# Attention's opening written out by hand: loads in order of need, block means spread by VectorE

## The chip, the core and the metric

The program runs on one core of a Trainium2 chip. A core has TensorE (PE: weight loads and matmuls), VectorE (DVE), ScalarE (ACT), GpSimd (POOL) and SyncE (SP), which here only issues transfers; 16 DMA engines move data between the device's memory and the on-chip buffers (SBUF; matmuls write to PSUM). The metric is the device time of one execution in microseconds (us), as a median over runs.

## The reference

Three layers in a row, in float32. The first is attention of 2 batches, 8 heads, 768 positions, 64 values per head, in which each query sees its near keys and one summary per block of 32 keys:

```
k_sum = k.reshape(B, H, nb, block, D).max(axis=3)
v_sum = v.reshape(B, H, nb, block, D).mean(axis=3)
scores_l = where(|i - j| < 16, scale * q @ k.T, -1e9)
scores_s = scale * einsum('bhsd,bhnd->bhsn', q, k_sum) + log(block)
a = softmax(concatenate([scores_l, scores_s], axis=-1))
out = a @ concatenate([v, v_sum], axis=2)
```

Its output goes through a mixture of 8 experts, of which each token takes its best (`relu(x @ w1[e]) @ w2[e]`, times a gate), and then through `(x @ w_a * (x @ w_b)) @ w_out`.

## The kernel before

Heads are taken two at a time: a **pair** p is 128 partitions of keys, and there are 8 pairs, p0 to p7 (4 for each batch). A pair's 768 queries are 12 windows of 64; four windows are a **quad**, so there are 24 quads, 0 to 23. Of the first batch, quads 0 to 2 belong to p0, 3 to 5 to p1, then p2 and p3 alternate (6, 8, 10 and 7, 9, 11); the second batch repeats this with p4 to p7 from quad 12 on.

A pair needs four loads, all issued on SP's queue: `kr` (keys, 400 KB), `qd` (queries, 384 KB), `vbt` (values laid out for block sums, 390 KB) and `vt` (values by window, 585 KB, 96 of 120 rows). They have 3, 3, 2 and 3 buffers. From `kr`, `key_blocks` takes the maxima over blocks of 32 (tile `ks`, one VectorE reduction). From `vbt`, `value_sums` makes sums in three additions on GpSimd, `value_blocks` turns them into means (one small matmul into `o`, a VectorE copy into `vs`), and `fill_v` spreads the 24 rows of `vs` over the 12 windows of `vt`, rows 96 to 119, by a DMA of 24 x 12 pieces of 520 bytes that SP issues.

A quad i then goes through: `windows` (three copies into `kt`: ScalarE from `kr`, VectorE from `kr`, VectorE or GpSimd from `ks`), `scores` (matmuls s<-kt,qd: s(i)), `largest` (four VectorE pieces, mask and maximum, in the trace the operation CUSTOM_DVE_ANT_0; the mask lies in `cs`), `exps` (ScalarE), `turn` (transposes into `pst`, ScalarE copy into `pt`), `values` (matmuls o<-vt,pt) and `norm` (three VectorE instructions, rs, rs and x). The results of `values` and of `value_blocks` share two PSUM buffers; scores have three, transposes two.

The order on each engine is the order in which the code calls these helpers (a manual schedule). `step(n)` interleaves stages of several quads: in step n, windows of quad n+3, norm of n-2, exps of n+1, scores and largest of n+2, turn of n and values of n-1; helpers of pairs and loads are called in the steps ahead of the pair's first quad. Engines and queues work their own instructions off in order, so an instruction that waits holds what stands behind it on its engine. When a group of quads is done, its rows are turned and routed (px, pl, prb), and the expert stage begins as soon as its tokens are known.

Of the kernel before, what the change touches and what calls it, by code (L numbers as in the profile page):

```python
# [10 lines left out]
F32 = mybir.dt.float32  # L11
# [7 lines left out]
ALU = mybir.AluOpType  # L19
AX = mybir.AxisListType  # L20
# [81 lines left out]
def fused_kernel(  # L102
# [276 lines left out]
    krs, qs, vbs, kss, vss, kts, vts, prs, nms, pts, os_, xt2 = ({} for _ in range(12))  # L379
    qds = [big.tile([P, QW, NWIN], F32, name=f"qd{i}") for i in range(NQD)]  # L380

    def load_k(p):
        kr = krs[p] = k_p.tile([P, S + 32], F32, name="kr")
        nc.sync.dma_start(kr, k[p])

    def load_vb(p):
        vbt = vbs[p] = v_p.tile([KW, 8, 2 * VW], F32, name="vbt", bufs=2)
        nc.sync.dma_start(vbt, vb[p])

    def load_q(p):  # L390
        qd = qs[p] = qds[len(qs) % NQD]
        nc.sync.dma_start(qd, q[p].rearrange("h d q n -> (h d) q n"))

    def load_v(p):
        vt = vts[p] = v_p.tile([KC, NWIN, 2 * VW], F32, name="vt")
        nc.sync.dma_start(vt[0:KW], v[p])

    def fill_v(p):
        nc.sync.dma_start(vts[p][KW:KC], vss[p][KW:KC].to_broadcast([NBLK, NWIN, 2 * VW]))

    n1 = CCOL["first"][1]
    nc.scalar.dma_start(cs[:, :n1], cst[:, :n1])

    zrow = big.tile([P, KD], F32, name="zrow")
    nc.gpsimd.memset(zrow, 0.0)
    nc.gpsimd.dma_start(xs[0:1, :].rearrange("a (p c) -> (a p) c", p=P), zrow)

    oh = r1.tile([P, NT, E], BF16, name="oh")
    unit = r1.tile([P, NT], F32, name="unit")
# [8 lines left out]

    def key_blocks(p):
        ks = kss[p] = s_p.tile([P, NBLK], F32, name="ks")  # L420
        nc.vector.tensor_reduce(
            out=ks, in_=krs[p][:, 16:16 + S].rearrange("p (m i) -> p m i", i=32), op=ALU.max, axis=AX.X)

    def value_sums(p):
        vbt = vbs[p]
        for r in (4, 2, 1):
            nc.gpsimd.tensor_tensor(out=vbt[:, 0:r], in0=vbt[:, 0:r], in1=vbt[:, r:2 * r], op=ALU.add)

    def value_blocks(p):
        o = ps_c.tile([P, 512], F32, name="o", tag="c")  # L430
# [42 lines left out]
    def exps(i):  # L473
        for w in range(4):
            nc.scalar.activation(prs[i][:, w, :], prs[i][:, w, :], AF.Exp, scale=-1.0, bias=nms[i][:, w:w + 1])
# [377 lines left out]
    def step(n):  # L853
        def ok(i):
            return 0 <= i < NQ

        def due(ahead):

            m = n + ahead
            return begin.get(0 if m == 1 else m) if m else None  # L860

        win = windows(n + 3) if ok(n + 3) else iter(())
        nrm = norm(n - 2) if ok(n - 2) else iter(())
        for ops in 3 * (win, nrm):
            next(ops, None)
        if ok(n + 1):
            exps(n + 1)
        if ok(n + 2):
            scores(n + 2)
            largest(n + 2)  # L870
        if n + 5 in begin:
            key_blocks(begin[n + 5])
        if due(3):
            value_sums(due(3))
        if ok(n):
            turn(n)
        if ok(n - 1):
            values(n - 1)
        if due(2):
            value_blocks(due(2))  # L880
        if due(1):
            fill_v(due(1))
        for ahead, load in ((5, load_q), (5, load_vb), (3, load_v), (7, load_k)):
            if n + ahead in begin:
                load(begin[n + ahead])
        for fn in todo.pop(n, []):
            fn()

    def wi(j):
        return lambda n: widx[:, j, n:n + 1]  # L890

    with tc.manual_schedule():
        for n in range(-7, NQ + 2):
            step(n)
            if n == 4:
                nc.scalar.dma_start(cs[:, n1:], cst[:, n1:])
                nc.scalar.dma_start(wg_sb, wg)
            if n == 8:
                nc.vector.tensor_copy(tri, cc("tri"))
# [350 lines left out]
```

## Time and profile before

| | us |
|---|---|
| median of 3 runs | 584.59 (583.51 to 589.82) |
| the profiled execution, its own time | 580.55 |
| its span in the trace | 578.8 |
| TensorE busy in the span | 542.7 (94%) |
| VectorE, ScalarE, GpSimd busy | 364.5, 245.9, 210.7 |

Attention and its routing fill about the first 100 us of the span, experts the stretch to 260 us, the last layer the rest. The trace is of the profiled execution; its own time lies 1.75 us above its span, and 4.04 us below the median of the runs.

### The profile page before, as it was taken

What the parts mean: (1) busy time and instruction counts of PE and PEld (TensorE: products, weight loads), DVE (VectorE), ACT (ScalarE), POOL (GpSimd) and SP (SyncE); (2) the same over time, 40 slices, a digit from 0 to 9 for tenths busy, and PEclk for the clock granted to TensorE, in tenths of its full rate; (3) what the DMA queues carried; (4) which work ended last, traced back from release to release, by engine and by line L of the source; (5) the groups of instructions that cost most, each with busy time, mean ns of one, the idle gap of its engine ahead of it and who ended that gap; (6) DMA issues with size and microseconds to landing.
All of it is one profiled execution on the core that took longest, in us unless ns stands there. A gap on an engine that the chain in (4) does not pass through costs nothing.

```text
span 578.8 us, 9146 instructions
## 1 busy us (share of the span) xinstructions
PE 542.7 (94%) x3358; PEld 451.7 (78%) x3358; DVE 364.5 (63%) x908; ACT 245.9 (42%) x516; POOL 210.7 (36%) x189
## 2 busy tenths in 40 slices
PE   4899976987979999999999999999999999999996
PEld 3678765967878997987778878888788888888885
DVE  3766676775767878777655766676667666342321
ACT  3667756345655655564422332233223322222321
POOL 3332337326164654740015334533453345200000
PEclk9999999999999999999999999999999999999999
DMA  8999883049684938554313231323132312020202
GB/s 255 253 218 278 219 302 148 8 176 336 247 310 172 375 131 323 207 230 166 124 37 109 74 107 39 109 74 106 40 110 72 108 39 74 1 74 0 74 0 74
DMA packets 24288, 83.88 MB, mean 145 GB/s; under 512 B 2864, under 2 KB 5424, under 8 KB 20656
## 3 DMA queue, kind: packets, MB, share of 16 engines
q1 hardware_dynamic: 13984, 38.16, 22.9%
q0 software_dynamic: 6944, 38.80, 17.6%
q10 hardware_dynamic: 3312, 6.29, 3.1%
q8 instruction: 28, 0.46, 0.3%
q14 instruction: 20, 0.16, 0.1%
HBM read 69.72 MB, written 12.32 MB: 142 GB/s over the span
## 4 chain that ended last, share of the span: by engine, by line
PE 50%; DVE 2%; DMA 1%; SPq 1%; ACT 0%; issue 0%; POOL 0%; POOLq 0%; DVEq 0%
PE pa L1124 11%; PE pa L1126 11%; PE pa L1125 11%; PE po L1156 6%; PE po L1157 6%; PE po L1155 6%; DMA yg<-ya 1%; PE px L988 1%; SPq L977 1%; DVE yg L978 0%; DVE c_top L1031 0%; DVE yw L990 0%; POOL yw L1032 0%; ACT yw L989 0%; DVE c_top L1024 0%
## 5 line engine op out<-in xcount | busy, mean ns | idle before, releaser
L1124 PE MATMUL pa<-yw,abh 128*128 128x512 f32 x288 | 113.7, 395 | 0.3 <-DVE yw L990 0.3
L1126 PE MATMUL pa<-yw,abl 128*128 128x512 f32 x288 | 112.6, 391 | 0.0
L1125 PE MATMUL pa<-yw,abh 128*128 128x512 f32 x288 | 112.2, 390 | 0.0
L1029 POOL TENSOR_TENSOR c_rest<-c_rest,c_ex 128x512 f32<-128x512 f32 x36 | 51.7, 1448 | 127.1 <-DVE c_ex L1028 126.4
L205 DVE TENSOR_TENSOR w<-w,w 128x512 fp32r<-128x512 f32 x100 | 69.1, 735 | 5.2 <-ACT w L204 3.5
L1126 PEld LDWEIGHTS pa<-yw,abl 128*128 128x128 f32 x288 | 54.0, 188 | 12.1
L1124 PEld LDWEIGHTS pa<-yw,abh 128*128 128x128 f32 x288 | 54.2, 188 | 11.5 <-DVE yw L990 0.5
L1125 PEld LDWEIGHTS pa<-yw,abh 128*128 128x128 f32 x288 | 54.1, 188 | 11.4
L277 PE MATMUL ph<-xh,w 128*128 128x256 f32 x192 | 55.0, 286 | 6.9 <-DVE hl L281 4.4
L204 ACT CAST w<-w 128x512 fp32r<-128x512 f32 x100 | 56.4, 619 | 3.9 <-DVE w L205 3.9
L1156 PE MATMUL po<-yw,gh 128*128 128x512 f32 x144 | 56.9, 395 | 0.2
L1155 PE MATMUL po<-yw,gh 128*128 128x512 f32 x144 | 56.2, 390 | 0.0
L1157 PE MATMUL po<-yw,gl 128*128 128x512 f32 x144 | 56.1, 390 | 0.0
L278 PE MATMUL ph<-xl,w 128*128 128x256 f32 x192 | 54.0, 281 | 0.0
L279 PE MATMUL ph<-xh,w 128*128 128x256 f32 x192 | 53.8, 280 | 0.0
L455 PE MATMUL s<-kt,qd 64*64 64x120 f32 x384 | 34.6, 324 | 9.5 <-DMA qd<-in_q 7.7
L277 PEld LDWEIGHTS ph<-xh,w 128*128 128x128 f32 x192 | 36.2, 189 | 9.1 <-DVE hl L281 5.4
L253 PE MATMUL py<-w,hh 128*128 128x512 f32 x104 | 41.0, 395 | 1.1 <-DVE w L205 1.1
L252 PE MATMUL py<-w,hh 128*128 128x512 f32 x104 | 41.8, 402 | 0.0
L1110 DVE TENSOR_TENSOR gl<-gt,gh 128x512 fp32r<-128x512 f32 x24 | 16.5, 691 | 40.0 <-ACT gh L1109 38.0
L1014 ACT ACTIVATE c_rest<-raw 128x512 f32<-128x512 uint32 x36 | 23.1, 670 | 42.8 <-POOL abl L1032 42.8
L254 PE MATMUL py<-w,hl 128*128 128x512 f32 x104 | 40.9, 393 | 0.0
(200 smaller groups left out, 1034.4 us busy)
## 6 DMA issues: line engine op xcount, KB each, us to landing
raw<-in_wab SPq DMA_DIRECT2D x22, 512.0 KB, 3.6
raw<-in_wc SPq DMA_DIRECT2D x12, 512.0 KB, 3.5
vt<-in_v SPq DMA_DIRECT2D x8, 585.0 KB, 8.7
kr<-in_k SPq DMA_DIRECT2D x8, 400.0 KB, 7.4
vbt<-in_vb SPq DMA_DIRECT2D x8, 390.0 KB, 9.7
qd<-in_q SPq DMA_DIRECT2D x8, 384.0 KB, 8.1
xs<-x ACTq DMA_DIRECT2D x12, 256.0 KB, 3.4
yg<-ya SPq DMA_DIRECT2D x8, 256.0 KB, 2.6
```

The source lines that it names most:

```text
L204: nc.scalar.copy(a[:, c], r[:, c])
L205: nc.vector.tensor_tensor(out=l[:, c], in0=r[:, c], in1=f(a[:, c]), op=ALU.subtract)
L277: nc.tensor.matmul(ph, a, xh[:, c, :], start=(c == 0), stop=False)
L278: nc.tensor.matmul(ph, a, xl[:, c, :], start=False, stop=False)
L279: nc.tensor.matmul(ph, l, xh[:, c, :], start=False, stop=(c == KD - 1))
L1029: nc.gpsimd.tensor_tensor(out=rest, in0=rest, in1=ex.bitcast(F32), op=ALU.mult)
L1124: nc.tensor.matmul(pa, a, yh[:, c, :], start=(c == 0), stop=False)
L1125: nc.tensor.matmul(pa, a, yl[:, c, :], start=False, stop=False)
L1126: nc.tensor.matmul(pa, l, yh[:, c, :], start=False, stop=(c == KD - 1))
L1155: nc.tensor.matmul(po[g][i], a, bh, start=(fc == 0), stop=False)
L1156: nc.tensor.matmul(po[g][i], a, bl, start=False, stop=False)
L1157: nc.tensor.matmul(po[g][i], l, bh, start=False, stop=(fc == KF2 - 1))
```

## The change

The steps -7 to 2, in which the pipeline filled by itself, give way to a function `prologue` that calls the helpers one by one, and the loop begins with step 3, in which `step` leaves out the norm and values that are done by then. In it:

- the load of p0's keys is cut in two, and so is the reduction of its block maxima;
- SP issues kr, qd and the constants `cs` of p0 first (`cs` came on ScalarE's queue), then vbt and vt of p0, then p1's loads;
- quads 0, 1, 2 are scored one after the other and go through turn and values before quad 3 is scored; `value_sums` of p0 is done by VectorE;
- `fill_v` is, for all 8 pairs, a VectorE copy of 24 x 1560 elements with a repeated source;
- the row of zeros that GpSimd writes out is made on one partition (1 x 512) and no longer on 128 (128 x 4).

```diff
-    def load_k(p):
+    def load_k(p, *at):
         kr = krs[p] = k_p.tile([P, S + 32], F32, name="kr")
-        nc.sync.dma_start(kr, k[p])
+        for a, b in zip((0, *at), (*at, S + 32)):
+            nc.sync.dma_start(kr[:, a:b], k[p][:, a:b])
...
     def fill_v(p):
-        nc.sync.dma_start(vts[p][KW:KC], vss[p][KW:KC].to_broadcast([NBLK, NWIN, 2 * VW]))
+        nc.vector.tensor_copy(vts[p][KW:KC], vss[p][KW:KC].to_broadcast([NBLK, NWIN, 2 * VW]))
...
-    nc.scalar.dma_start(cs[:, :n1], cst[:, :n1])
-
-    zrow = big.tile([P, KD], F32, name="zrow")
+    zrow = big.tile([1, DM], F32, name="zrow")
     nc.gpsimd.memset(zrow, 0.0)
-    nc.gpsimd.dma_start(xs[0:1, :].rearrange("a (p c) -> (a p) c", p=P), zrow)
+    nc.gpsimd.dma_start(xs[0:1, :], zrow)
...
     def key_blocks(p):
         ks = kss[p] = s_p.tile([P, NBLK], F32, name="ks")
-        nc.vector.tensor_reduce(
-            out=ks, in_=krs[p][:, 16:16 + S].rearrange("p (m i) -> p m i", i=32), op=ALU.max, axis=AX.X)
+        n = 1 if start[p] else 2
+        for i in range(n):
+            a, b = S // n * i, S // n * (i + 1)
+            nc.vector.tensor_reduce(
+                out=ks[:, a // 32:b // 32], in_=krs[p][:, 16 + a:16 + b].rearrange("p (m i) -> p m i", i=32),
+                op=ALU.max, axis=AX.X)
...
-            nc.gpsimd.tensor_tensor(out=vbt[:, 0:r], in0=vbt[:, 0:r], in1=vbt[:, r:2 * r], op=ALU.add)
+            (nc.gpsimd if start[p] else nc.vector).tensor_tensor(out=vbt[:, 0:r], in0=vbt[:, 0:r], in1=vbt[:, r:2 * r], op=ALU.add)
...
+    def prologue():
+
+        p0, p1, p2, p3 = list(start)[:4]
+        load_k(p0, 16 + S // 2)
+        load_q(p0)
+        nc.sync.dma_start(cs[:, :n1], cst[:, :n1])
+        load_vb(p0)
+        load_v(p0)
+        load_k(p1)
+        load_q(p1)
+        load_vb(p1)
+        load_k(p2)
+        load_v(p1)
+        key_blocks(p0)
+        for i in range(3):
+            list(windows(i))
+        for i in range(2):
+            scores(i)
+            largest(i)
+            exps(i)
+        value_sums(p0)
+        scores(2)
+        largest(2)
+        turn(0)
+        value_blocks(p0)
+        fill_v(p0)
+        turn(1)
+        exps(2)
+        values(0)
+        turn(2)
+        list(norm(0))
+        values(1)
+        key_blocks(p1)
+        list(windows(3))
+        values(2)
+        list(norm(1))
+        scores(3)
+        largest(3)
+        list(windows(4))
+        exps(3)
+        value_sums(p1)
+        scores(4)
+        largest(4)
+        value_blocks(p1)
+        key_blocks(p2)
+        list(windows(5))
+        fill_v(p1)
+        load_k(p3)
+        for p in (p2, p3):
+            load_q(p)
+            load_vb(p)
+
     with tc.manual_schedule():
-        for n in range(-7, NQ + 2):
+        prologue()
+        for n in range(3, NQ + 2):
+            if n == 4:
+                key_blocks(list(start)[3])
             step(n)
```

SP's queue, its first transfers, before (the number behind a tile's name is that of the tile made; kr_148, qd0, vbt_153 and vt_161 are p0's; vt_161<-vs_215 is the spreading of p0's means):

```order
L384 DMA kr_148<-in_k 128x800
L392 DMA qd0_131<-in_q 128x768
L388 DMA vbt_153<-in_vb 96x1040
L384 DMA kr_155<-in_k 128x800
L396 DMA vt_161<-in_v 96x1560
L392 DMA qd1_132<-in_q 128x768
L388 DMA vbt_188<-in_vb 96x1040
L384 DMA kr_217<-in_k 128x800
L399 DMA vt_161<-vs_215 24x12x130
L396 DMA vt_253<-in_v 96x1560
L384 DMA kr_255<-in_k 128x800
```

The same queue now (kr_147, qd0, vbt_152 and vt_154 are p0's; L900 is the load of the constants):

```order
L385 DMA kr_147<-in_k 128x400 x2
L393 DMA qd0_131<-in_q 128x768
L900 DMA cs_60<-in_cst 128x512
L389 DMA vbt_152<-in_vb 96x1040
L397 DMA vt_154<-in_v 96x1560
L385 DMA kr_156<-in_k 128x800
L393 DMA qd1_132<-in_q 128x768
L389 DMA vbt_159<-in_vb 96x1040
L385 DMA kr_161<-in_k 128x800
L397 DMA vt_163<-in_v 96x1560
```

The spreading of p0's means no longer stands ahead of p1's vt, the constants stand third, and p0's vt ahead of p1's keys.

TensorE's first matmuls before (s_167, s_198, s_227 are quads 0 to 2, s_265 and s_318 are 3 and 4; o<-vbt is a pair's block means, o<-vt,pt are a quad's values):

```order
L455 MATMUL s_167<-kt_157,qd0_131 64x120 x8
L455 MATMUL s_198<-kt_163,qd0_131 64x120 x8
L431 MATMUL o_213<-vbt_153,cs_60 24x130
L455 MATMUL s_227<-kt_190,qd0_131 64x120 x8
L480 MATMUL pst_245<-cs_60,pr_176 120x128 x4
L455 MATMUL s_265<-kt_219,qd1_132 64x120 x8
L480 MATMUL pst_282<-cs_60,pr_207 120x128 x4
L491 MATMUL o_289<-vt_161,pt_250 64x65 x8
L431 MATMUL o_298<-vbt_188,cs_60 24x130
L455 MATMUL s_318<-kt_257,qd1_132 64x120 x8
```

And now (s_180, s_199, s_221 are quads 0 to 2, s_309 and s_335 are 3 and 4):

```order
L458 MATMUL s_180<-kt_168,qd0_131 64x120 x8
L458 MATMUL s_199<-kt_172,qd0_131 64x120 x8
L458 MATMUL s_221<-kt_176,qd0_131 64x120 x8
L483 MATMUL pst_236<-cs_60,pr_189 120x128 x4
L434 MATMUL o_243<-vbt_152,cs_60 24x130
L483 MATMUL pst_248<-cs_60,pr_208 120x128 x4
L494 MATMUL o_259<-vt_154,pt_241 64x65 x8
L483 MATMUL pst_268<-cs_60,pr_230 120x128 x4
L494 MATMUL o_280<-vt_154,pt_253 64x65 x8
L494 MATMUL o_295<-vt_154,pt_273 64x65 x8
L458 MATMUL s_309<-kt_291,qd1_132 64x120 x8
L458 MATMUL s_335<-kt_324,qd1_132 64x120 x8
```

All of p0's transposes and values stand ahead of quad 3's scores now; from quad 6 on the row is the one of before.

VectorE where p3's means are copied out, between the maxima of quad 7 and of quad 8, before:

```order
L433 COPY vs<-o 24x130
L500 TENSOR_SCALAR rs<-o 128x4
L443 COPY kt<-kr 128x4x32
L502 RECIPROCAL rs<-rs 128x4
L504 TENSOR_TENSOR x<-o,rs 128x2x128
L462 ISA pr,nm<-s,cs 128x120
```

And now:

```order
L436 COPY vs<-o 24x130
L400 COPY vt<-vs 24x1560
L503 TENSOR_SCALAR rs<-o 128x4
L446 COPY kt<-kr 128x4x32
L505 RECIPROCAL rs<-rs 128x4
L507 TENSOR_TENSOR x<-o,rs 128x2x128
```

The copy that spreads a pair's means (here p2's) stands ahead of a quad's norm, whose last instruction frees the PSUM buffer that the next values write to.

## Rows read from the trace of the kernel before

**Rows 1.** The span in stretches: busy time of each engine, clock, DMA.

```profile
core 0: us, PE busy (x) PEld busy (x) DVE busy (x) ACT busy (x) POOL busy (x), PEclk, DMA share, GB/s
0.00:7.70 7.70, 0.00 (x0) 0.02 (x1) 1.58 (x6) 2.30 (x4) 1.36 (x7) 1.00 0.76 242
...
14.10:24.40 10.30, 9.83 (x131) 8.17 (x130) 8.99 (x51) 8.05 (x24) 3.12 (x6) 1.00 1.01 246
24.40:32.20 7.80, 5.18 (x56) 3.71 (x56) 2.44 (x19) 3.79 (x11) 5.43 (x10) 0.78 1.03 250
32.20:67.30 35.10, 35.10 (x471) 28.99 (x470) 25.33 (x155) 25.95 (x75) 7.92 (x12) 1.00 1.01 254
67.30:84.00 16.70, 12.28 (x164) 10.50 (x162) 10.99 (x75) 8.72 (x25) 6.30 (x7) 1.00 0.70 232
```

**Rows 2.** TensorE in order of time, 7 to 38 us: start, duration, [idle before <-releaser].

```profile
7.71 3.50 PE L455 MATMUL s<-kt,qd 64*64 64x120 f32 x32 [7.71 <-DMA qd<-in_q]
...
14.10 1.33 PE L455 MATMUL s<-kt,qd 64*64 64x120 f32 x16
15.36 0.65 PE L480 MATMUL pst<-cs,pr 128*120 128x128 f32 x4
...
26.16 0.71 PE L491 MATMUL o<-vt,pt 120*64 120x65 f32 x16 [1.80 <-DMA vt<-vs]
...
27.59 1.89 PE L455 MATMUL s<-kt,qd 64*64 64x120 f32 x16
29.41 1.11 PE L480 MATMUL pst<-cs,pr 128*120 128x128 f32 x4
...
34.75 1.35 PE L455 MATMUL s<-kt,qd 64*64 64x120 f32 x16
```

**Rows 3.** All engines in order of time, 0 to 30 us.

```profile
5.26 0.95 DVE L421 TENSOR_REDUCE ks<-kr 128x24 f32<-128x768 f32 x1 [4.24 <-DMA kr<-in_k]
...
6.13 0.22 DVE L443 COPY kt<-kr 128x128 f32<-128x128 f32 x1
...
9.64 0.28 DVE L462 CUSTOM_DVE_ANT_0 pr<-s,cs 128x120 f32<-128x120 f32 x1 [2.98 <-PE s L455]
...
10.46 0.95 DVE L421 TENSOR_REDUCE ks<-kr 128x24 f32<-128x768 f32 x1
...
14.28 2.60 POOL L427 TENSOR_TENSOR vbt<-vbt 96x520 f32<-96x520 f32 x3 [2.44 <-DMA vbt<-in_vb]
...
14.45 1.21 DVE L443 COPY kt<-kr 128x128 f32<-128x128 f32 x1
```

**Rows 4.** SP's issues of transfers in order of time.

```profile
12.70 1.00 SPq L399 DMA_DIRECT2D vt<-vs  x1
...
57.29 0.83 SPq L399 DMA_DIRECT2D vt<-vs  x1
...
58.80 0.52 SPq L388 DMA_DIRECT2D vbt<-in_vb  x1
```

**Rows 5.** DMA, 14 to 16 us.

```profile
DMA packets 346, 0.34 MB, mean 168 GB/s; under 512 B 20, under 2 KB 308, under 8 KB 346
```

**Rows 6.** DMA, 9 to 13 us.

```profile
DMA packets 329, 1.09 MB, mean 273 GB/s; under 512 B 43, under 2 KB 43, under 8 KB 329
```

**Rows 7.** DMA, 0 to 6 us, in 40 slices of 0.15 us.

```profile
GB/s 0 0 0 0 0 0 0 0 0 0 0 85 85 107 128 212 274 280 167 280 280 342 385 266 414 383 463 383 405 480 349 437 413 420 382 408 388 347 326 194
```

**Rows 8.** VectorE's instructions by line and shape: busy us, mean ns.

```profile
L205 DVE TENSOR_TENSOR w<-w,w 128x512 fp32r<-128x512 f32 x100 | 69.1, 735 | 5.2 <-ACT w L204 3.5
...
L1022 DVE TENSOR_SCALAR c_ex<-raw 128x512 int32<-128x512 int32 x36 | 15.1, 420 | 0.0
...
L504 DVE TENSOR_TENSOR x<-o,rs 128x256 f32<-128x256 f32 x24 | 10.2, 424 | 0.4
...
L433 DVE COPY vs<-o 24x130 f32<-24x130 f32 x8 | 2.4, 300 | 6.9 <-PE o L431 6.8
L445 DVE COPY kt<-ks 128x96 f32<-128x96 f32 x13 | 2.3, 180 | 0.0
```

**Rows 9.** TensorE in order of time, 64 to 102 us.

```profile
71.25 0.40 PE L431 MATMUL o<-vbt,cs 96*24 96x130 f32 x2 [1.36 <-POOL vbt L427]
```

More of the change, by code (lines that the diff above doesn't have):

```diff
@@ L862, in step @@
         win = windows(n + 3) if ok(n + 3) else iter(())
-        nrm = norm(n - 2) if ok(n - 2) else iter(())
+        nrm = norm(n - 2) if n > 3 and ok(n - 2) else iter(())
         for ops in 3 * (win, nrm):
@@ L876, in step @@
             turn(n)
-        if ok(n - 1):
+        if n > 3 and ok(n - 1):
             values(n - 1)
```

## The prediction

> **What bounds the kernel now.** The table of stretches comes first [rows 1]. From 32.2 to 67.3 us TensorE is busy all 35.10 us at full clock: there attention runs at TensorE's pace, and nothing that another engine or a transfer saves counts. Before that it isn't so: nothing until 7.7 us, 9.83 of 10.30 us from 14.1, and only 5.18 of 7.80 from 24.4, at a granted clock of 0.78. After it, 12.28 of 16.70. So the change can win in the first 32 us and behind 67 us, and what it wins there moves everything behind it, since experts and last layer start from attention's rows.
>
> TensorE in order of time says what ends each pause [rows 2]. Its first matmul starts at 7.71 us, when the queries have landed. At 26.16 it has stood 1.80 us for `vt<-vs`, the DMA that spreads p1's means. Behind that pause the clock is low: s and pst of a quad take 1.89 and 1.11 us against 1.33 and 0.65 at 14.1, so 1.0 us is lost again. At 71.25 it has stood 1.36 us for the block sums of the last pair [rows 9].
>
> The DMA engines' share is 1.0 from 14 to 67 us at 246 to 254 GB/s [rows 1], against 273 GB/s from 9 to 13 us [rows 6]. Over 14 to 16 us, while p0's spreading runs in its 288 pieces of 520 bytes, 0.34 MB move at 168 GB/s [rows 5]; at 273 it would be 0.55. One spreading so costs the loads about 0.8 us; there are eight. SP waits too: its spreading goes out at 12.70, after p0's means exist, and all later loads stand behind it [rows 4].
>
> **The change part by part.**
>
> *Start.* The bytes moved by time follow from the slices [rows 7]: 0.41 MB by 3.5 us, 0.67 MB by 4.2, 0.80 MB by 4.5. Before, keys and constants (0.67 MB together) share the engines and VectorE starts on the keys at 5.26 [rows 3], some 1.0 us after their last byte. Alone on the engines, the first half of the keys (0.2 MB, 2.9 us) would be usable at 3.9, the second at 4.5, the queries at 5.5. VectorE then needs half of 0.95 us for the second half's maxima and 0.22 us each for two copies: quad 0's scores start at 5.6 us in place of 7.71, 2.1 us sooner. If the early rate is a ramp that sharing has nothing to do with, it is 7.0.
>
> *First quads.* I walk the new order with durations of rows. At the start TensorE takes 1.75 us per quad of scores (3.50 for two [rows 2], against 1.33 later): quads 0 to 2 end at 10.8. VectorE has finished quad 1's maxima at 10.0 (four pieces take 0.82 us, 9.64 to 10.46 [rows 3]). It then makes p0's block sums: 520, 260 and 130 columns of two SBUF sources, by 0.735 us for 512 [rows 8] and in proportion about 1.45 us; quad 2's maxima to 12.3; the means' copy 0.30 [rows 8]; the spreading.
>
> *The spreading's price* isn't in the trace: 1560 elements from one source. Such copies take 0.18 us for 96 elements and 0.42 for 512 [rows 8], 0.58 ns an element: 1.0 us. The block maxima take 0.95 us for 768 elements [rows 3], by which it would be 1.9. I take 1.0, since the copy is of the first kind, and keep 1.9 as the bound. On the other side DMA and SP lose eight transfers.
>
> So the spreading ends at 13.65, quad 0's values (0.71 [rows 2]) at 14.4, its norm (0.75, of which the multiplication is 0.42 [rows 8]) at 15.4, p1's maxima (0.95) at 16.3, a copy into kt: quad 3 is scored at 16.7, where before it was 14.10 [rows 2]. The code then alternates: maxima of quad 3 (0.9) and the copy for quad 4 (0.22) stand ahead of quad 4's scores (19.3); maxima of 4, a means' copy (0.30), p2's maxima (0.95) and a copy stand ahead of quad 5's (22.9). TensorE stands 4.9 us in pieces from 11 to 23 us. From quad 6 on (24.8) it is fed: 28.1 for quad 7, 30.9 for quad 8, 33.9 for quad 9 with half a microsecond for values that wait till VectorE, late from p2's spreading, has freed their PSUM buffer. Before, quad 9 is at 34.75 [rows 2], and from here on both orders are alike. The 2.1 us of the start, the 1.80 of the spreading's DMA and the 1.0 of the low clock go into the serial opening; 0.85 us are left.
>
> *Middle.* VectorE is busy 25.33 of 35.10 us [rows 1]; p2's to p6's spreadings make it 30.3, so TensorE stays the bound (at 1.9 us each 34.8, which is just full).
>
> *Last pair.* SP held the last block sums' load until 58.80, behind a spreading that went out at 57.29 [rows 4]. Without eight spreadings at 0.8 us and that hold it lands some microseconds sooner, and the 1.36 us wait [rows 9] goes. Next late is VectorE, with two spreadings more in 67 to 84 us (10.99 of 16.70 busy [rows 1]): I charge 0.4 us. For clock lost in the pauses from 11 to 23 us I charge 0.3, a third of one low stretch of 1.0; zero and two stretches are the bounds.
>
> The rest has one answer: the larger zero row and the constants' place on SP cost nothing, since the mask is first used at 9.64 [rows 3], after the constants' bytes have long moved.
>
> Sum: -0.85 - 1.36 + 0.4 + 0.3 = -1.5 us. Against the profiled execution's 580.55 that is 579.0; the runs' median lies 4.04 above it, so **583.1**.
>
> **Rivals.**
>
> *VectorE and GpSimd keep each other out: slower.* At 14.45 a VectorE copy of 128 elements takes 1.21 us beside a GpSimd addition that began at 14.28, where the same copy took 0.22 at 6.13 [rows 3]; it stays until 15.66, while the additions run. The spreadings are such copies, and the new block sums on GpSimd run in the same stretch. If those of p1, p2 and p3 each wait 1.0 us where VectorE is already the chain (22 to 34 us), the sum turns to +1.5: **586.1**. It decides once two of them coincide with an addition. For it: p2's additions and p1's spreading both become ready at about 23 us. Against: a pair's own additions are over before its spreading. The Trainium skill says of this (SBUF — State Buffer, "SBUF: two separate sides") that VectorE and GpSimd share one pair of ports under an exclusive lock, held for a whole instruction. The row at 14.45 agrees with 1.21 us against 0.22.
>
> *The copy is slow: no change.* At 1.9 us the first spreading is 0.9 later on the chain, p2's and p3's stretch TensorE's wait by another 0.8, and VectorE, full in the middle, costs some 0.3: -1.5 + 2.0 = +0.5, **585.1**. Against it stand the two copies' rows. The Trainium skill (VectorE: DVE Perf Modes, "The perf-mode tier table") gives float32 copies within SBUF two elements a cycle; by that the price would be about 0.9 us, as the rows have it.
>
> *The order of loads brings nothing: no change.* If the first bytes come no faster alone, the start gives 0.7 and not 2.1: -0.1, **584.5**. For it: only 85 to 280 GB/s move until 3 us [rows 7], though two queues have work.
>
> *Everything fits: faster.* If no low stretch comes and GpSimd's and VectorE's pieces interleave without the half microsecond, and the clock also holds in 67 to 101 us: -0.85 - 0.5 - 1.36 - 1.5 = -4.2, **580.4**; with the start's waits of 4.9 us a third smaller, 578.8.
>
> **How the numbers follow.** Forecast 583.1: chance 0.45. Slower by the ports 0.15, slow copy 0.12, loads alike 0.13, all fits 0.15. A measurement of this kernel tells about 1% (5.8 us) from no change; the three runs span 1.1%. Below 578.7 lies a third of the last case and a little of the spread of runs, 0.09; above 590.4 only an unforeseen wait, 0.06; within 0.85. The range goes from 578.0, which leaves out only the far end of the last case, to 588.0: the ports' case with the clock's two low stretches on top of it (586.1 + 1.7).
>
> **What would show it.** In the changed profile: TensorE's first s at 5.3 to 6.0 us; the spreading as a VectorE row of 24x1560 at 0.9 to 1.1 us; pauses of TensorE of 1 to 2 us ahead of quads 4 and 5; quad 9's scores at 33 to 35 us; no row of 520-byte DMAs; no wait for the last block sums near 70 us. Wrong would be: a spreading of over 1.5 us or one that waits for GpSimd (ports, slow copy), a first s at 7 us (loads), or a clock below 1.0 in more than one stretch of the first 35 us.

## The result, and the profile after

Over 20 runs each, side by side, the changed kernel takes 587.13 us (median; 580.56 to 593.43) and the kernel before 584.95 us (574.57 to 589.82); the ratio is 1.0141, 95% interval 1.0108 to 1.0174. Both were measured again twice, on chips where runs spread less: 578.50 against 575.00 us (ratio 1.0060, 1.0033 to 1.0088) and 578.24 against 575.12 us (1.0050, 1.0030 to 1.0071). So the change costs 3.1 and 3.5 us there, 0.5 to 0.6%, and 1.4% by the ratio of the first comparison, where 1.5 us of gain was forecast. Disturbed executions, over 1.5% longer than the same kernel's fastest, are left out of the ratios, of the table of experiments and of the profile, so the trace shown here is not that of the first profiled execution after the change (593.43 us) but `c_after2`, a later run of the same kernel (578.59 us, span 576.8).

The stretches of [rows 1] in that trace (the columns are those of [rows 1]), and the routing behind them:

```profile
core 0: us, PE busy (x) PEld busy (x) DVE busy (x) ACT busy (x) POOL busy (x), PEclk, DMA share, GB/s
0.00:7.70 7.70, 1.83 (x18) 1.86 (x20) 1.87 (x8) 2.40 (x4) 1.95 (x8) 1.00 0.75 218
...
14.10:24.40 10.30, 6.17 (x92) 5.14 (x92) 6.58 (x29) 4.98 (x16) 3.78 (x8) 0.89 1.04 274
24.40:32.20 7.80, 7.80 (x78) 6.12 (x76) 6.51 (x33) 4.18 (x12) 5.97 (x10) 0.71 1.01 262
32.20:67.30 35.10, 34.58 (x462) 28.66 (x462) 29.13 (x150) 26.61 (x75) 11.25 (x13) 1.00 0.81 231
67.30:84.00 16.70, 13.51 (x197) 11.24 (x195) 15.24 (x96) 10.70 (x30) 5.11 (x5) 1.00 0.49 179
84.00:101.00 17.00, 10.81 (x118) 8.17 (x115) 12.94 (x31) 8.96 (x21) 9.87 (x9) 0.80 0.51 184
```

Against [rows 1], TensorE loses the stretch 14.1 to 24.4 us (6.17 busy for 9.83), and in the next one it is busy all the time, yet at a granted clock of 0.71. The DMA share falls from 1.01 to 0.81 behind 32 us, where the spreadings' small pieces no longer run. VectorE from 67.3 to 84 us is nearly full: 15.24 of 16.70, for 10.99. But the 10.99 are those of one trace. In `c_before`, a second trace of the kernel before, VectorE is as full there as after the change (15.71):

```profile
67.30:84.00 16.70, 15.40 (x221) 12.80 (x220) 15.71 (x107) 11.90 (x32) 7.67 (x9) 1.00 0.77 236
```

TensorE in order of time in `c_after2`, the opening (answers to [rows 2]):

```profile
5.87 5.09 PE L458 MATMUL s<-kt,qd 64*64 64x120 f32 x48 [5.87 <-DMA qd<-in_q]
...
13.94 0.70 PE L494 MATMUL o<-vt,pt 120*64 120x65 f32 x16 [1.02 <-ACT pr L478]
...
16.86 1.33 PE L458 MATMUL s<-kt,qd 64*64 64x120 f32 x16 [0.22 <-POOL kt L448]
19.54 1.35 PE L458 MATMUL s<-kt,qd 64*64 64x120 f32 x16 [1.34 <-DVE kt L446]
...
23.78 1.89 PE L458 MATMUL s<-kt,qd 64*64 64x120 f32 x16 [2.56 <-DVE kt L446]
25.60 1.11 PE L483 MATMUL pst<-cs,pr 128*120 128x128 f32 x4
26.64 1.89 PE L458 MATMUL s<-kt,qd 64*64 64x120 f32 x16
...
30.26 1.33 PE L458 MATMUL s<-kt,qd 64*64 64x120 f32 x16
...
35.64 1.35 PE L458 MATMUL s<-kt,qd 64*64 64x120 f32 x16
```

These are quads 0 to 2, then 3, 4, 5, 6, 7 and 9. Quad 0 starts 1.84 us before [rows 2], quad 3 2.76 us behind it, and quad 9 0.89 us behind: 11 us lie between the scores of quad 0 and of quad 3, 6.4 before. The DMA wait of 1.80 us is gone, pauses of 1.02, 1.34 and 2.56 us are there instead, and behind them quads 5 and 6 run at half clock (1.89 and 1.11 us for 1.33 and 0.65).

The end of attention, TensorE's waits (answers to [rows 9]), then VectorE and GpSimd beside the last of them:

```profile
75.48 1.36 PE L458 MATMUL s<-kt,qd 64*64 64x120 f32 x16 [0.83 <-DVE kt L448]
79.13 1.33 PE L458 MATMUL s<-kt,qd 64*64 64x120 f32 x16 [1.04 <-DVE kt L448]
...
95.27 1.19 PE L494 MATMUL o<-vt,pt 120*64 120x65 f32 x16 [4.70 <-DVE x L507]
```

```profile
86.00 7.94 DVE L633 TENSOR_TENSOR ga<-ga,d 128x2 f32<-128x2 f32 x1
86.53 7.38 POOL L202 TENSOR_TENSOR w<-w,w 128x512 fp32r<-128x512 f32 x6
```

The wait for the last block sums is gone. Quads 21 and 22 wait for VectorE instead, whose copies stand behind the spreadings of p6 and p7. The two rows at 86 us are taken up at the end.

The DMA view of 14 to 16 us (answers to [rows 5]):

```profile
DMA packets 158, 0.54 MB, mean 272 GB/s; under 512 B 21, under 2 KB 21, under 8 KB 158
```

0.54 MB in place of 0.34, as forecast, at the rate of [rows 6]. VectorE's new instruction, grouped by shape (the columns of [rows 8]):

```profile
L400 DVE COPY vt<-vs 24x1560 f32<-24x1560 f32 x8 | 7.9, 984 | 0.3
```

### The profile page after: what moved, and what is told of

It reads as the page before. It is cut to its first block, busy times and chain, and to the rows that moved or that the text cites. A ratio compares the mean times of both kernels' runs of the same rounds, so it can differ in the third digit from the quotient of the medians.

```text
span 591.6 us, 9129 instructions
## 1 busy us (share of the span) xinstructions
PE 548.4 (93%) x3358; PEld 457.1 (77%) x3358; DVE 373.4 (63%) x920; ACT 247.0 (42%) x516; POOL 204.3 (35%) x186
## 3 DMA queue, kind: packets, MB, share of 16 engines
q10 hardware_dynamic: 3168, 6.03, 2.9%
## 4 chain that ended last, share of the span: by engine, by line
PE 49%; DVE 2%; DMA 1%; SPq 0%; ACT 0%; issue 0%; POOL 0%; POOLq 0%; DVEq 0%
PE pa L1182 11%; PE pa L1184 11%; PE pa L1183 10%; PE po L1214 6%; PE po L1215 6%; PE po L1213 6%; DMA yg<-ya 1%; PE px L1046 1%; SPq L1035 0%; DVE yg L1036 0%; DVE c_top L1089 0%; DVE yw L1048 0%; POOL yw L1090 0%; ACT yw L1047 0%; DVE c_top L1082 0%
## 5 line engine op out<-in xcount | busy, mean ns | idle before, releaser
L277 PE MATMUL ph<-xh,w 128*128 128x256 f32 x192 | 56.2, 293 | 12.4 <-DVE hl L281 7.7
L279 PE MATMUL ph<-xh,w 128*128 128x256 f32 x192 | 55.1, 287 | 0.4 <-issue 0.4
L281 DVE SCALAR_TENSOR_TENSOR hl<-ph,hh 128x256 fp32r<-128x256 f32 x48 | 19.8, 418 | 37.5 <-ACT hh L280 34.8
L252 PE MATMUL py<-w,hh 128*128 128x512 f32 x104 | 43.0, 413 | 0.0
L458 PEld LDWEIGHTS s<-kt,qd 64*64 64x64 f32 x384 | 29.8, 229 | 16.3 <-issue 10.5
L253 PE MATMUL py<-w,hh 128*128 128x512 f32 x104 | 41.7, 401 | 0.0
```

What stands on the lines that cost most here:

```text
L277: nc.tensor.matmul(ph, a, xh[:, c, :], start=(c == 0), stop=False)
L279: nc.tensor.matmul(ph, l, xh[:, c, :], start=False, stop=(c == KD - 1))
L458: nc.tensor.matmul(s[d, w, :], qs[b, c][d, :, 4 * t2 + w], kts[i][d, w, :], start=True, stop=True)
```

## Experiments

The table has the start of TensorE's first matmul of each step (us) in every trace but the first after the change, and the median less that of the kernel before, measured side by side. "Product" is the first matmul of the experts. Beside `after_old_loads`, `best`, `best_start` and `best_warm` the kernel before itself ran from 573.60 to 593.27 us; there the steps in the trace say more than the medians.

| kernel | quad 0 | quad 3 | quad 9 | quad 23 | product | median |
|---|---|---|---|---|---|---|
| before, first trace | 7.71 | 14.10 | 34.75 | 83.40 | 101.4 | |
| c_before | 7.97 | 13.94 | 35.21 | 81.01 | 103.2 | -0.1 |
| c_after | 6.82 | 18.73 | 38.28 | 84.83 | 107.0 | +3.5 |
| c_after2 | 5.87 | 16.86 | 35.64 | 82.94 | 105.3 | +3.1 |
| before_fill_dve | 7.79 | 15.30 | 33.37 | 80.19 | 102.6 | 0.0 |
| before_loads | 5.81 | 16.34 | 37.73 | 83.03 | 105.2 | +2.9 |
| before_loads_fill | 7.25 | 17.47 | 35.93 | 82.71 | 104.9 | +1.7 |
| hybrid | 6.84 | 17.27 | 35.36 | 80.17 | 102.7 | +0.4 |
| after_fill_dma | 6.53 | 25.06 | 49.17 | 94.48 | 116.7 | +13.4 |
| after_old_loads | 7.82 | 18.80 | 38.31 | 85.46 | 105.8 | +11.3 |
| after_quad3_first | 5.72 | 14.99 | 37.52 | 84.34 | 106.9 | +5.1 |
| after_warm | 5.87 | 17.98 | 37.11 | 84.40 | 106.8 | +5.2 |
| after_warm_less | 6.08 | 17.31 | 35.99 | 82.39 | 104.8 | +2.5 |
| after_warm_fit | 6.27 | 17.09 | 34.77 | 81.68 | 103.9 | +2.1 |
| after_two_dma | 6.48 | 17.47 | 36.21 | 81.69 | 103.9 | +1.9 |
| best | 7.46 | 14.00 | 31.93 | 79.93 | 98.2 | -1.7 |
| best2 | 7.47 | 13.29 | 31.94 | 77.48 | 99.7 | -2.7 |
| best_start | 7.23 | 15.94 | 35.40 | 83.10 | 100.9 | +3.8 |
| best_warm | 7.51 | 13.52 | 31.64 | 79.58 | 107.8 | +17.9 |

**Both kernels again, unedited.**

c_before: 

> The kernel before once more, for a second trace of it. By the theory that the later loss (expert stage, first product to first matmul of the last layer: 170.3 us in the trace of before, 180.0 in that of after) is a spread that both kernels have, a second trace may show anything from 170 to 180 us there, and other stretches at half clock than the first. By the theory that it belongs to the change, it shows 170 to 172 again. The attention part repeats either way: quad 9's scores at 34.6 to 34.9 us, s of quad 23 at 83 to 84.

c_after: 

> The changed kernel once more, for a second trace. The opening should repeat within 0.2 us (quad 9's scores at 36.2 to 36.6, a stretch at half clock of 7 to 10 us from about 19 us). If the expert stage's 180.0 us belong to the change, they come again within 2 us; if they are a spread of both kernels, 170 to 180.

c_after2: 

> The changed kernel a third time, as the control of this call: quad 9's scores at 36.2 to 38.5 us (36.41 and 38.28 in the first two traces), half clock for 10 to 14 us between 15 and 33 us.

The opening repeats only roughly: quad 9 of the changed kernel comes at 36.41 (the first trace), 38.28 and 35.64 us, that of the kernel before at 34.75 and 35.21. In `c_after` a stretch at half clock starts as early as 15.2 us, before quad 3; that and a start 0.95 us later than in `c_after2` make its 18.73. From the first product to the last layer the experts take 162.4 us in `c_before`, 163.3 in `c_after`, 164.2 in `c_after2`. The 170.3 and 180.0 of the first two traces didn't come again for either kernel, so a difference of 10 us there is none of the change; 0.9 and 1.8 us are left, whose cause wasn't looked for. In `c_before`, TensorE's wait for the last block sums, the 1.36 us of [rows 9], is 0.23 us.

**The spreading alone.**

```diff
-        nc.sync.dma_start(vts[p][KW:KC], vss[p][KW:KC].to_broadcast([NBLK, NWIN, 2 * VW]))
+        nc.vector.tensor_copy(vts[p][KW:KC], vss[p][KW:KC].to_broadcast([NBLK, NWIN, 2 * VW]))
```

before_fill_dve: 

> The kernel before with the spreading by VectorE alone, its loads and steps as they were. By the theory that the serial opening is the loser: the wait of 1.80 us for the DMA at 26 us and the half clock behind it go, VectorE's 1.02 us per pair is covered from 35 to 67 us, the wait for the last block sums falls by about 1.4; quad 9's scores at 33.0 to 33.8 (before 34.75) and a median 2 to 4 us below that of before. By the rival that VectorE's spreadings are the loser (they make VectorE late for a quad's maxima): quad 9 at 34.8 to 35.8 and a median 0 to 3 us above before.

In the old steps VectorE's copy wins 1.84 us at quad 9 (33.37 for 35.21), as the first theory had it, and the median is the same as before (ratio 0.9996, 0.9972 to 1.0021). TensorE waits here as in `c_after2`:

```profile
72.73 1.35 PE L455 MATMUL s<-kt,qd 64*64 64x120 f32 x16 [0.83 <-DVE kt L445]
76.37 1.33 PE L455 MATMUL s<-kt,qd 64*64 64x120 f32 x16 [1.04 <-DVE kt L445]
```

and VectorE, third of the busy columns, by stretch in `c_before` and then in `before_fill_dve`:

```profile
60.00:67.00 7.00, 7.00 (x99) 5.75 (x98) 4.49 (x27) 6.11 (x19) 2.43 (x3) 1.00 1.03 285
67.00:76.00 9.00, 8.63 (x123) 7.01 (x121) 8.20 (x53) 5.92 (x18) 3.82 (x5) 1.00 0.57 132
```

```profile
60.00:67.00 7.00, 6.50 (x94) 5.49 (x94) 6.70 (x37) 5.94 (x18) 4.06 (x5) 1.00 0.64 161
67.00:76.00 9.00, 7.50 (x106) 6.13 (x104) 7.69 (x44) 5.14 (x15) 2.90 (x3) 1.00 0.19 56
```

From 60 to 67 us VectorE is full (6.70 of 7.00, for 4.49). Behind it, it is no busier than in `c_before` (7.69 of 9.00, for 8.20), where it had little idle time already; but attention's last quads, two spreadings and the routing of the first batch stand on it in a row, and TensorE waits for the copies at the end of that row. What the opening wins is mostly given back there, 1.0 of 1.84 us by quad 23.

**The changed kernel with the spreading by DMA.** The same line, the other way round.

after_fill_dma: 

> The changed kernel with the spreading by DMA again. By the theory of the serial opening: p0's values wait for a DMA of about 2 us behind the means in place of a copy of 1.0, all of it on the chain, so quad 3 is scored about 1 us later than in after (17.9 for 16.92) and quad 9 at 37 to 39, the last pair's wait of about 1.4 us is back, median 1 to 4 us above after. By the rival (VectorE's copies are the loser): quad 9 at 35 to 36 and a median 1 to 2 us below after.

```profile
20.95 1.16 PE L494 MATMUL o<-vt,pt 120*64 120x65 f32 x16 [7.55 <-issue]
```

Quad 0's values wait 7.55 us, not the 2 that I expected: the transfer stands behind all loads that the opening has issued by then (SP issues it at 13.53 us, its pieces of 520 bytes move from 17.7). Quad 9 comes at 49.17 us. The serial opening needs VectorE's copy; the copy doesn't need the serial opening.

**The loads.** `before_loads` issues the changed loads ahead of the old steps, the spreading by DMA:

```diff
+    early = [(load_k, p0), (load_q, p0), None, (load_vb, p0), (load_v, p0), (load_k, p1), (load_q, p1),
+             (load_vb, p1), (load_k, p2), (load_v, p1)]
...
+        for e in early:
+            if e is None:
+                nc.sync.dma_start(cs[:, :n1], cst[:, :n1])
```

before_loads: 

> The kernel before with the loads in the changed order alone (p0's keys in two halves, constants third on the queue, p0's values ahead of p1's keys, the small row of zeros), steps and the spreading by DMA as before. By the theory that the loads give what they promised and the serial opening spends it: scores of quad 0 at 6.2 to 6.8 us (7.97 in the second trace of before), quad 9 0.5 to 1.5 us earlier than 35.2. By the rival that a gain of the start is lost to the spreading's DMA in any order, since p1's values and keys are queued ahead of it now: quad 9 at 35 to 37, the wait for the DMA near 17 to 26 us as long as before or longer.

`before_loads_fill` has VectorE's spreading besides, so all of the change but the serial opening.

before_loads_fill: 

> The same with the spreading by VectorE: everything of the change but the serial opening. By the theory of the serial opening: quad 9's scores at 32.0 to 33.2 us, no half clock before 35 us, 3 to 5 us ahead of after there; behind 67 us VectorE with the last two spreadings gives 1 to 2 us back, as in the kernel with the spreading alone, so a median 0.5 to 2.5 us below before and 4 to 6 below after. If the serial opening is not the cause, it comes within 1 us of after.

Both miss. Quad 0 starts earlier (5.81 and 7.25 us), and quad 3 later than in the old order: 17.47 for 15.30 with VectorE's spreading. VectorE in `before_loads_fill`, p1's block maxima:

```profile
13.38 0.95 DVE L423 TENSOR_REDUCE ks<-kr 128x24 f32<-128x768 f32 x1 [3.29 <-DMA kr<-in_k]
```

p1's keys are the load that the pipelined steps wait for, and p0's values stand ahead of them now; in `before_fill_dve` the same row begins at 10.86. So the changed loads cost quad 9 2.56 us there (35.93 for 33.37). In the median they cost 1.7 us with VectorE's spreading (1.7 for 0.0) and 2.9 with the DMA's. `best_start` below shows that the place of p0's values isn't all of it.

`after_old_loads` completes the square: serial opening, VectorE's spreading, the loads of before.

after_old_loads: 

> The changed kernel with the loads of the kernel before (p0's keys in one piece, constants on ScalarE's queue, p1's keys ahead of p0's values, the row of zeros on 128 partitions): the serial opening and VectorE's spreading alone. In the pipelined steps the new order of loads cost quad 9 2.6 us, since p1's keys come later. If that cost belongs to the loads themselves, it goes here too: quad 9 at 35.5 to 37 us for 38.28, median 1 to 3 us below after. If the serial opening hides it, since p1's keys are needed only after p0's values there, the later start of quad 0 (about 1 us) remains: quad 9 at 38.5 to 39.7, median 0 to 2 us above after.

Quad 3 at 18.80, 10.98 us behind quad 0 as in `c_after2` and `after_two_dma` (10.99; 11.91 in `c_after`, with its stretch at half clock). The opening's chain runs from quad 0 on, so here an earlier quad 0 counts and p1's keys don't. With VectorE's spreading throughout, quad 9 is at 33.37 us (old steps, old loads), 35.93 (old steps, new loads), 38.31 (serial, old loads) and 35.64 to 38.28 (serial, new loads). The serial opening costs 4.9 us there with the old loads, and between nothing and 2.4 with the new ones. The new loads help only a chain that starts with quad 0 and needs p1's keys late; in the old steps they cost.

**The serial order and the clock.** In `after_quad3_first` only quad 3 is moved forward:

```diff
         value_blocks(p0)
+        key_blocks(p1)
+        list(windows(3))
         fill_v(p0)
         turn(1)
+        scores(3)
         exps(2)
         values(0)
         turn(2)
+        largest(3)
         list(norm(0))
         values(1)
```

after_quad3_first: 

> The changed kernel with one thing moved: p1's block maxima and quad 3's windows stand ahead of the spreading of p0's means on VectorE, quad 3's scores ahead of quad 0's values on TensorE, and its maxima ahead of quad 0's norm. If the order of VectorE's chain is what the opening loses: quad 3 scored at 15 to 16 us for 18.73, quad 4 at 19 to 20 for 21.40, quad 9 1.5 to 2.5 us earlier than in the changed kernel of the same call, median 1 to 2.5 us below it. If it is the clock alone: quad 9 within 0.7 us of it, since the pauses stay.

```profile
14.99 1.89 PE L458 MATMUL s<-kt,qd 64*64 64x120 f32 x16 [2.40 <-POOL kt L448]
...
21.31 1.35 PE L458 MATMUL s<-kt,qd 64*64 64x120 f32 x16 [0.38 <-DVE kt L446]
```

A miss: quad 3 comes at 14.99, but quad 4 at 21.31 (19.54 in `c_after2`), since p0's values now stand behind quad 3's scores on TensorE (16.81 us for 13.94), and with them p0's norms on VectorE, which stand ahead of quad 4's windows as before; and TensorE ran at half clock from 13.9 us. One quad moved out of the row doesn't make it a pipeline.

`after_warm` gives TensorE matmuls with unused results in the pauses (`warm` writes them to the PSUM tile that the real matmuls overwrite); `after_warm_less` has half as many, `after_warm_fit` 2, 2, 5 and 10:

```diff
+    def warm(t, i, n):
+        b, c, t2 = quads[i]
+        for _ in range(n):
+            nc.tensor.matmul(t[0:D, 0:KC], qs[b, c][0:D, :, 0], kts[i][0:D, 0, :], start=True, stop=True)
...
-        value_blocks(p0)
+        value_blocks(p0, 2)
...
-            scores(n + 2)
+            scores(n + 2, {5: 10}.get(n + 2, 0))
```

after_warm: 

> The changed kernel with TensorE fed in the opening's pauses: 34 matmuls of 64x120 whose results are overwritten (4 ahead of p0's means, 6 ahead of quad 0's values, 8 ahead of quad 4's scores, 13 ahead of quad 5's, 3 ahead of quad 6's), each batch a little shorter than the pause in the trace of after. By the theory that the opening loses by the clock as much as by the pauses: no stretch at half clock before 35 us, scores of quads 4, 5, 6 and 8 at 1.33 us for 1.89, quad 9 at 35.5 to 36.7 us (38.28 in the second trace of after), and a median 1 to 2.5 us below after. By the rival that VectorE's chain alone sets the pace: the clock is full, but quad 9's scores stay within 0.5 us of 38.28 and so does the median.

after_warm_less: 

> The changed kernel with half the fillers (2, 3, 5, 7 and 2 matmuls in place of 4, 6, 8, 13 and 3), so that each batch ends before what TensorE waits for is there. If the half clock costs what its rows suggest (0.56 us for each of quads 4, 5, 6, 0.46 for two transposes, 0.2 to 0.3 for others): clock full to 35 us, quad 9 1.5 to 2.5 us earlier than in the changed kernel of the same call, median 0.5 to 2 us below it. If the clock is only a companion of the pauses: quad 9 less than 1 us earlier.

after_warm_fit: 

> The changed kernel with fillers of 2, 2, 5 and 10 matmuls ahead of p0's means, quad 0's values, quad 4's and quad 5's scores, and none elsewhere. If the half clock is a cost of its own: scores of quads 5 and 6 at 1.33 us and not 1.89, quad 9 less quad 3 at 17.0 to 17.8 us (18.8 to 19.6 in three traces of the changed kernel), median 1 to 2 us below it (578.2 to 578.5, where before had 575.0). If it is only a companion of the pauses: quad 9 less quad 3 at 18.3 or more.

With all fillers the clock is full up to 95 us, but they stand on the path themselves (those ahead of quad 0's values end 1.0 us after the spreading), and the kernel is slower still. With half of them a stretch at half clock remains from 24.9 to 28.3 us. Both are inconclusive. The fitted ones show the clock's share up to quad 9; TensorE there:

```profile
17.09 1.33 PE L465 MATMUL s<-kt,qd 64*64 64x120 f32 x16 [0.21 <-POOL kt L449]
...
24.02 1.35 PE L465 MATMUL s<-kt,qd 64*64 64x120 f32 x16
...
26.56 1.33 PE L465 MATMUL s<-kt,qd 64*64 64x120 f32 x16 [0.60 <-DVE nm L472]
...
34.77 1.35 PE L465 MATMUL s<-kt,qd 64*64 64x120 f32 x16
```

From quad 3 to quad 9 17.68 us, 1.1 to 1.9 less than in three traces of the changed kernel (18.78, 19.49, 19.55) and one with the same opening (`after_two_dma`, 18.74). So the half clock costs 1.1 to 1.9 us there. In the time of the whole kernel that isn't clear of the spread of runs: the median stands 2.1 us above before and not 3.1 to 3.5, but the ratio is 1.0048 (1.0028 to 1.0068) beside 1.0050 and 1.0060.

**The last two spreadings.** `hybrid` is `before_loads_fill`, `after_two_dma` the changed kernel, and `best` the kernel before, all three with this `fill_v`:

```diff
+        dst, src = vts[p][KW:KC], vss[p][KW:KC].to_broadcast([NBLK, NWIN, 2 * VW])
+        if start[p] < NQ - 6:
+            nc.vector.tensor_copy(dst, src)
+        else:
+            nc.scalar.dma_start(dst, src)
```

hybrid: 

> Everything of the change but the serial opening, and the spreadings of the last two pairs by DMA again, issued by ScalarE's queue and not by SP's. By the theory that VectorE is the bound from 60 to 82 us once all eight spreadings are on it: no wait of 0.8 to 1.0 us ahead of the scores of quads 21 and 22, s of quad 23 1.5 to 2.5 us earlier than with all eight on VectorE, a median 1 to 4 us below before. By the rival that this stretch is covered (what is gained there is lost in the routing, whose chain starts from the last rows of the first batch): quad 23 earlier, the first products of the experts within 0.5 us of those of the kernel with all eight.

after_two_dma: 

> The changed kernel with the spreadings of p6 and p7 by DMA from ScalarE's queue. If VectorE's lateness at the end of attention costs the changed kernel what it cost the pipelined one: no waits of 0.8 and 1.0 us ahead of quads 21 and 22, quad 9 to the first product of the experts 2 us shorter than the 68.1 to 69.7 us of its three traces, median 1 to 2.5 us below it, so within 2 us of before. If the routing behind it is set by another chain: the first product within 0.7 us and the median too.

best: 

> The kernel before, loads and steps untouched, the spreadings of p0 to p5 by VectorE and those of p6 and p7 by DMA from ScalarE's queue. From the kernel with all eight on VectorE it keeps the gain of the opening (quad 9 at 33.2 to 33.8), from the hybrid the last pair without VectorE's lateness: quad 23 at 77.8 to 78.8 us (81.01 in the second trace of before). If what is gained there also moves the end: median 1.5 to 3 us below before. If the routing behind it waits for something else (GpSimd's chain), 0 to 1 below.

best2: 

> Six spreadings by VectorE, the last two by DMA from ScalarE's queue, all else as before, a second time. If its first comparison (ratio 0.994) was the kernel and not the chip: quad 9 at 31.5 to 33.5, quad 23's scores at 78 to 80, median 2 to 4 us below before. If its gain at quad 9 is lost on the way: within 1 us of before.

From quad 9 to quad 23, `hybrid` takes 44.81 us where `before_loads_fill` takes 46.78, and `after_two_dma` 45.48 where the changed kernel takes 46.55 to 47.30. The waits of 0.83 and 1.04 us are gone. The first product comes 2.2 us earlier in `hybrid`; in `after_two_dma` it comes 67.7 us behind quad 9, less of a gain than the 2 us expected, but the median falls to 1.9 us above before (ratio 1.0039, 1.0021 to 1.0057). So by medians VectorE's two last spreadings cost 1.3 us in the pipelined steps and 1.2 to 1.6 in the changed kernel, each alone no more than the spread of the runs. `hybrid` itself is even with before (1.0001, 0.9976 to 1.0025), not below it.

`best` takes from the change only what paid. Its ratio to before is 0.9937 (0.9886 to 0.9987) on the chip with the wide spread and, as `best2`, 0.9952 (0.9929 to 0.9975): 572.43 against 575.12 us. It beats the kernel before by 0.5%, and the changed one by more. Beside `before_fill_dve` (0.0) it shows the last two spreadings once more, here at 2.7 us and clear of the spread. Quad 9 and quad 23 in `best2`:

```profile
31.94 1.35 PE L459 MATMUL s<-kt,qd 64*64 64x120 f32 x16
```

```profile
77.48 1.33 PE L459 MATMUL s<-kt,qd 64*64 64x120 f32 x16 [0.19 <-DVE kt L449]
```

**One edit at a time.** Four runs lead from the kernel before to the changed one by one edit each. Medians less that of the kernel before, each measured side by side with it, on three chips:

| step | edit | from | to | costs |
|---|---|---|---|---|
| before to `best2` | six spreadings by VectorE, two by ScalarE's queue | 0 | -2.7 | -2.7 |
| `best2` to `hybrid` | the changed loads | -2.7 | +0.4 | +3.1 |
| `hybrid` to `after_two_dma` | the serial opening | +0.4 | +1.9 | +1.5 |
| `after_two_dma` to the changed kernel | the last two spreadings by VectorE | +1.9 | +3.1, +3.5 | +1.2 to +1.6 |

The ratios go the same way: 0.9952 (0.9929 to 0.9975), 1.0001 (0.9976 to 1.0025), 1.0039 (1.0021 to 1.0057), then 1.0050 and 1.0060. The first two steps are clear of the spread of runs, the other two only just or not. The prices hold in this order alone: under the serial opening the changed loads save time (`after_old_loads`), in the old steps they cost.

**Two additions to best that fail.** `best_start` has the keys in halves and the constants third on SP's queue, but p1's keys ahead of p0's values:

```diff
+    early = [(load_k, p0), (load_q, p0), None, (load_vb, p0), (load_k, p1), (load_v, p0), (load_q, p1),
```

best_start: 

> The same with the early part of the changed loads (p0's keys in halves, constants third on SP's queue, small row of zeros) but p1's keys still ahead of p0's values. By the theory that the opening is bound by the arrival of p1's keys and not by quad 0: scores of quad 0 at 5.9 to 7.2 us, yet quad 3 and quad 9 within 0.4 us of those without it. By the rival that an earlier quad 0 moves everything: quad 9 about 1 us earlier, at 32.2 to 32.8.

Neither theory: quad 9 is 3.5 us later than in `best`. The first stretches in `best`, and then in `best_start`:

```profile
0.00:3.00 3.00, 0.00 (x0) 0.00 (x0) 0.18 (x2) 1.28 (x1) 1.07 (x6) 1.00 0.36 73
3.00:4.00 1.00, 0.00 (x0) 0.00 (x0) 0.00 (x0) 0.00 (x0) 0.00 (x0) 1.00 0.92 347
4.00:8.00 4.00, 0.54 (x6) 0.57 (x8) 1.41 (x4) 1.02 (x3) 0.30 (x1) 1.00 1.05 334
```

```profile
0.00:3.00 3.00, 0.00 (x0) 0.00 (x0) 0.18 (x2) 1.28 (x1) 1.44 (x6) 1.00 0.37 106
3.00:4.00 1.00, 0.00 (x0) 0.00 (x0) 0.76 (x2) 0.70 (x2) 0.00 (x0) 1.00 0.77 190
4.00:8.00 4.00, 0.77 (x8) 0.80 (x10) 0.71 (x4) 0.42 (x2) 0.30 (x1) 1.00 1.03 293
```

Quad 0's first keys land early, but with this order, all loads on one queue, only 190 GB/s move from 3 to 4 us for 347, and 293 for 334 up to 8 us. By 8 us that is 1.68 MB for 1.90 (rates by the lengths of the stretches). p1's maxima start at 11.71 us for 10.21 in `best`. So the changed loads cost the old steps as much with p1's keys ahead of p0's values as behind them. Whether it is the second queue or the halved rows wasn't tried apart.

`best_warm` adds fillers ahead of quad 22's values:

```diff
+        if n == NQ - 1:
+            warm(n, 24)
```

best_warm: 

> The kernel with the six and two spreadings, with 24 matmuls of 64x120 (some 4 us, results unused) ahead of quad 22's values, where TensorE stands 4.7 us for VectorE and runs at half clock for some 10 us behind it. If the clock is what the routing loses (22.2 us from quad 23's scores to the first product of the experts against 18.0 in the first trace of before, where the half clock lasted 3.4 us): the half clock between 88 and 102 us is gone, the first product 2 to 4 us earlier, median 2 to 4 below that without it. If VectorE's and GpSimd's chain sets that stretch: clock full, first product within 0.7 us.

A miss that tests little: in `best` on that chip the pause which they were to fill was 0.55 us, and not 4.7, so they stood on the path for 8.29 us, the last 5 of them at half clock.

## Why the prediction was wrong

*Start.* Half right: quad 0 at 5.87, 6.03 and 6.82 us for 5.6. What failed is that the rest of the edit to the loads costs nothing. By 7.7 us the changed kernel has moved 0.18 MB less than the kernel before (218 GB/s for 242), `best_start` 0.22 MB less than `best` by 8 us with p1's maxima 1.5 us later, and in the old steps the changed loads cost 3.1 us (`hybrid` for `best2`). Only under the serial opening does the earlier start reach quad 3 (16.86 us in `c_after2`, 18.80 in `after_old_loads`). Which part of the edit costs, the constants' place on SP or the halved keys, is open.

*First quads* is the step that turned the sign: "The 2.1 us of the start, the 1.80 of the spreading's DMA and the 1.0 of the low clock go into the serial opening; 0.85 us are left." None are left. The walk held up to quad 4 (16.86 and 19.54 us in `c_after2` for 16.7 and 19.3); quad 5 comes at 23.78 for 22.9. It failed at "From quad 6 on (24.8) it is fed": quad 6 at 26.64, quad 9 at 35.64 to 38.28 for 33.9. By `after_warm_fit`, with full clock quad 9 is at 34.77, 0.9 behind the walk; the clock makes 1.1 to 1.9 us of the rest. In place of the 0.85 us of gain there is a loss of 0.4 to 3.5 us against the two traces of before, and at full clock nothing (34.77 for 34.75 and 35.21). The gain of the spreading's DMA that the prediction counted on is real: `best2` keeps 2.7 us by leaving loads and steps alone.

*The clock*, charged with 0.3 us, bounds 0 and 2.0, costs 1.1 to 1.9 at quad 9: the term was mis-sized by a factor of four or more, though inside its bounds. It was priced as a third of one low stretch of the kernel before (3.4 us at half clock); the serial opening's pauses are followed by 7 to 14 us of it.

*The spreading's price* was right: 0.97 us in most cases, mean 0.98 for 1.0, though one of the "two copies" that it was read from, the row of 0.42 us, is a TENSOR_SCALAR. *Middle* too: VectorE 29.13 us of 35.10 for 30.3, TensorE 34.58.

*Last pair* failed too, by less. VectorE was charged with 0.4 us, since it was busy 10.99 of 16.70 us. That row doesn't repeat: in `c_before` the same stretch has 15.71, so there was hardly any idle time for two more spreadings, and they cost 1.2 to 1.6 us. The 1.36 us on the other side was no stable gain either: the same wait is 0.23 us in `c_before`.

So the sum splits in two. With the last two spreadings left to DMAs, the forecast's terms give -0.85 + 0.3 - 1.36 = -1.9 us; `after_two_dma`, which is that kernel, takes 1.9 us more than before. For those two on VectorE the forecast adds 0.4, the runs 1.2 to 1.6. The sign was lost in the opening, loads and steps together; the end of attention made the loss larger. What in the opening costs the 1.9 us, beyond the clock, is not placed to the microsecond: quad 9 of one kernel differs by 2.6 us between traces.

*Rivals.* Loads that bring nothing: not so for quad 0; in the old steps they bring worse than nothing, since p1's keys come later. The slow copy: no. Of VectorE and GpSimd keeping each other out, the place was right and the price small. At 24.78 us in `c_after2` the copy of 128 elements behind p1's spreading takes 1.19 us for 0.22, beside GpSimd's additions of p2 (24.00 to 27.18), once and not three times. In the pipelined steps the first spreading itself takes 1.75 to 2.03 us beside such additions (`before_loads_fill`, `hybrid`, `best2`), yet quad 9 is at 31.94 in `best2` and at 31.93 in `best`, where it takes 0.97. "Everything fits" is the kernel `best`, which needed the old loads and the old steps for it; the 1.5 us that this case takes off for the clock behind 67 us come from no row.

## What to carry to other kernels

Price an order of steps by its chain through all engines up to the point where both orders are alike again, at the clock that its pauses leave: here a start 1 to 2 us earlier bought a chain of 11 us in place of 6.4. Before work is moved to an engine, read its idle time around the place where it will stand, and in more than one trace: 10.99 of 16.70 us in the first was 15.71 in the second. A change that bundles three edits is worth taking apart: here one of the three paid, in six of its eight places.

## What the runs showed that was not expected

VectorE's product of 128 by 2 elements (`ga`) takes 7.94 us in `c_after2`: it ends only when GpSimd's row of six subtractions beside it ends (7.38 us, without a gap). In the first trace of before:

```profile
86.47 3.06 DVE L630 TENSOR_TENSOR ga<-ga,d 128x2 f32<-128x2 f32 x1
86.99 5.07 POOL L202 TENSOR_TENSOR w<-w,w 128x512 fp32r<-128x512 f32 x4
```

There GpSimd's second subtraction ends at 89.50 and the third begins at 89.56, since ScalarE's piece for it is ready at 89.49; `ga` ends at 89.52, in that gap. In `best` the same happens at 86.04 to 86.08. How long VectorE stands is so decided by whether GpSimd runs out of input for 0.05 us. Where it does, quad 23's scores to the first product take 18.0 and 18.2 us; in `c_before`, where `ga` takes 7.93, TensorE stands 4.69 us, then runs 10.2 us at half clock, and it is 22.2. The Trainium skill (SBUF — State Buffer, "SBUF: two separate sides") says that the port pair which VectorE and GpSimd share is held for a whole instruction; these rows show a wait over up to six of them. It strikes both kernels: `ga` takes 7.92 to 7.95 us in all 14 traces from chips where runs spread little, and 2.75 to 5.50 in the six others. So it is no part of the 3.1 and 3.5 us. No run here removed it; it is the next thing to try, at up to 4 us by the first product.
